# The gated stage's first product in 2x2 blocks: seven block products instead of eight

## The chip, the cores and the metric

The kernel runs on one NeuronCore of a Trainium2 chip. The metric is the device time of one execution in microseconds (us). The engines are TensorE (PE in the rows, with its weight loads as PEld), VectorE (DVE), ScalarE (ACT), GpSimd (POOL) and SyncE (SP), which here only issues transfers. Each engine takes its instructions in the order in which the program lists them.

## What is computed

Three layers follow one another on 8 sequences of 576 tokens with 512 features: an attention by landmarks, a mixing layer (Fourier transform, normalization, two products with 2048 hidden features), and the gated layer that the change touches. Of the reference, cut to that layer:

```python
B, S, D = x.shape                       # 8, 576, 512;  d_ff = 1024
x_prev = np.concatenate([np.zeros((B, 1, D)), x[:, :-1, :]], axis=1)
xk = mu_k * x + (1.0 - mu_k) * x_prev
xr = mu_r * x + (1.0 - mu_r) * x_prev
k = np.maximum(xk @ w_k, 0.0)           # first product
v = k * k @ w_v                         # second product
r = 1.0 / (1.0 + np.exp(-(xr @ w_r)))   # gate
return r * v
```

## The kernel before

The 4608 tokens are worked in 9 blocks of 512. Two stages follow one another. In the first, the attention of the 8 sequences (`batch`) is laid between the products of the mixing layer (`block_a`, 9 blocks). In the second, the gated stage, a class `Gated` holds one block's work.

Every number that goes into a product is held as two fp16 halves, high and low, and each product is made of three matmuls (`PARTS`: high by high, high by low, low by high). The first product of a block is `first(f)` for f = 0 to 7: 128 of the 1024 hidden features, 4 chunks of the 512 input features, 3 parts, so 12 matmuls of 128x512 into one PSUM bank (`ph`, two banks in turn). ScalarE evacuates the bank with a Relu (`rk`), VectorE squares, ScalarE and VectorE split the square into halves (`k2`). `second(f)` takes them up two steps later with 12 matmuls into the four `acc` banks, and `gate(j)` is 12 more, four times a block, into a bank of the pool `gp`. At the end of a block VectorE multiplies each `acc` by the gate (`o`), and it is stored. `prep(i)` makes the operands `xk` and `xr` of a block: it loads `yb`, squares (`sq`), sums over features through four transposes, gets a power of two as scale, spreads it by four more transposes (`rs`), mixes each token with the one before it (`xt`), and splits the result into halves.

The weights come as 64 bit floats. In the first stage `Weights.run` takes apart a piece of 128x512 of them at a time (tile `wst`; three ScalarE and two VectorE instructions), and keeps `w_k`, `w_v` and `w_r` as fp16 halves in HBM; the gated stage loads them back.

The order on each engine is not the order of the code. A class `Plan` records all instructions, and `issue()` lists them by a planner with costs of its own (`Engine.cost`): at each point an engine takes the instruction that the planner holds ready and that has the longest way to the end (`key`, to which `iss.lead` adds: `NOW` for the stage's products, `SOON` for `prep`, 0 for the far weights). The block matmuls alone keep the order of the code (`chain=True`). The lines 333 (matmul), 349 (transpose), 317 (DMA) and 188 (the other engines) in the rows are those of helpers, so instructions are told apart by their tiles.

Of the kernel before, what the change touches and what calls it, by code (L numbers as in the profile page):

```python
# [11 lines left out]
F32 = mybir.dt.float32  # L12
# [11 lines left out]
DM = H * D  # L24
# [500 lines left out]
class Weights:  # L525
# [11 lines left out]
    def clear(self, x):  # L537
        self.iss.g.memset(x, 0)
        return x

    def run(self, src, hi, lo, room=None):

# [502 lines left out]
def build(nc, tc, a):  # L1045
# [5 lines left out]
    with stack, tc.manual_schedule():  # L1051
# [67 lines left out]
            w12_items += [piece("w_ch2", f, 0, w2, f) for f in range(4 * g, 4 * g + 4)]  # L1119


        shapes = {"w_k": [128, 2, 4, FF2], "w_v": [128, 2, 8, DM], "w_r": [128, 2, 4, DM]}
        kept = {
            n: iss.dram(tc.dram_tile(x, F16, name="d" + n), x, F16, "d" + n)
            for n, x in shapes.items()
# [6 lines left out]
                kept[name][:, :, rows, c:c + WCH],  # L1132
            )

        far_items = [far("w_k", c, g) for g in range(2) for c in range(4)]
        far_items += [far("w_v", f, 0) for f in range(8)] + [far("w_r", c, 0) for c in range(4)]

        def tmp(name="tmp"):
            return iss.tile(com, [128, 512], F32, name, "tmp", 3)
# [146 lines left out]
        for n, x in enumerate(w12_items):  # L1286
            weights.run(*x, room=rooms[n % 3] if n < 24 else None)
        iss.lead = 0.0
        for x in far_items:
            weights.run(*x)  # L1290
        iss.slack = 0.0
# [14 lines left out]
        wk, wv, wr = ([ws[n][:, x] for x in range(2)] for n in ("w_k", "w_v", "w_r"))  # L1306
        mus = iss.tile(pb, [128, 4, 4], F32, "mus")
        iss.load(mus[:, 0], a["mu_k"])
        iss.load(mus[:, 1], a["mu_r"])
# [2 lines left out]

        def prep(i):
            iss.lead = SOON
            pool, nb, nx = (pb2, 2, 8) if i else (pb, 1, 4)
            y = iss.tile(pool, [128, 4, BLK + 1], F32, "yb", bufs=nb)
            if i == 0:
                g_.memset(y[:, :, 0:1], 0.0)
                iss.load(y[:, :, 1:], ys[:, :, 0:BLK])
            else:  # L1320
                iss.load(y, ys[:, :, BLK * i - 1:BLK * i + BLK])
            q = None
            for c in range(0, 4, 2):
                pair = []
                for d in (c, c + 1):
                    pair.append(iss.tile(pool, [128, BLK + 1], F32, "sq", bufs=3))
# [30 lines left out]
            xk = [iss.tile(pool, [128, 4, BLK], F16, "xk", f"xk{x}", nb) for x in "hl"]  # L1357
            xr = [iss.tile(pool, [128, 4, BLK], F16, "xr", f"xr{x}", nb) for x in "hl"]
            for c in range(4):
                for n, x in enumerate((xk, xr)):  # L1360
                    t = iss.tile(pool, [128, 512], F32, "xt", bufs=nx)
                    s_.activation(t, y[:, c, 0:BLK], AF.Copy, scale=mus[:, 2 + n, c:c + 1])
                    if i < B:
                        g_.memset(t[:, o:o + 1], 0.0)
                    v_.scalar_tensor_tensor(
                        t, y[:, c, 1:], mus[:, n, c:c + 1], t, op0=ALU.mult, op1=ALU.add
                    )
                    v_.tensor_tensor(t, t, rs, op=ALU.mult)
                    s_.activation(x[0][:, c], t, AF.Copy)
                    g_.tensor_tensor(x[1][:, c], t, x[0][:, c], op=ALU.subtract)  # L1370
            return xk, xr, nz, qi

        class Gated:


            def __init__(self, i):
                self.i = i
# [14 lines left out]
                s_.activation(e, ps, AF.Sigmoid, scale=self.nz[:, j:j + 1])  # L1392
                self.sg.append(e)

            def first(self, f):
                iss.lead = NOW
                ps = ph()
                sl = slice(128 * f, 128 * f + 128)
                for c in range(4):
                    for n, (x, y) in enumerate(PARTS):  # L1400
                        mm(
                            ps, wk[x][:, c, sl], self.xk[y][:, c],
                            c == 0 and n == 0, c == 3 and n == 2, chain=True,
                        )
                rk = iss.tile(pb2, [128, 512], F32, "rk", bufs=3)
                s_.activation(rk, ps, AF.Relu, scale=1.0 / (4 * WS))
                k2 = iss.tile(pb2, [128, 2, 512], F16, "k2", bufs=4)
                v_.tensor_tensor(rk, rk, rk, op=ALU.mult)
                s_.activation(k2[:, 0], rk, AF.Copy)
                v_.tensor_tensor(k2[:, 1], rk, k2[:, 0], op=ALU.subtract)  # L1410
                self.ks[f] = k2

            def second(self, f):
                iss.lead = NOW
                if f == 0:
                    self.acc = acc_banks()
                k2 = self.ks.pop(f)
                for j in range(4):
                    sl = slice(128 * j, 128 * j + 128)
                    for n, (x, y) in enumerate(PARTS):  # L1420
                        mm(
                            self.acc[j], k2[:, x, sl], wv[y][:, f],
                            f == 0 and n == 0, f == 7 and n == 2, chain=True,
                        )
                if f < 7:
                    return
                for j in range(4):
                    o = iss.tile(pb2, [128, 512], F32, "o", bufs=3)
# [5 lines left out]
                    iss.load(a["out"][r0:r0 + 128, :], o)  # L1434


        blocks = {}
        for n in range(8 * NB + 2):
            i, f = divmod(n, 8)
            if i < NB:  # L1440
                if f == 0:
                    blocks[i] = Gated(i)
                blocks[i].first(f)
            if n >= 2:
                blocks[(n - 2) // 8].second((n - 2) % 8)
            if i < NB and 1 <= f < 5:
                blocks[i].gate(f - 1)
        iss.issue()


# [87 lines left out]
```

## Time and profile before

| | |
|---|---|
| median of three runs | 1510.58 us (1510.31 to 1510.58) |
| span of the profiled execution | 1508.6 us |
| instructions on the engines | 21555 |
| busy PE / PEld / DVE / ACT / POOL | 1495.0 / 734.4 / 822.5 / 601.2 / 291.2 us |
| the gated stage, first to last matmul | 1028.9 to 1503.9 us |

The span is from the first to the last instruction in the trace; no device time of its own is listed for the profiled execution, and the median lies 2.0 us above its span. Matmuls are pipelined, and a row's duration of one matmul overlaps the next one's, so their pace is read from the starts of two runs of matmuls in a timeline and not from the mean duration.

### The profile page before, as it was taken

The page shows a single profiled execution, that of the slowest core. Times are in us where ns is not written, and L with a number is a line of the kernel's source. Part 1 is how long each engine was busy: PE and PEld are TensorE (multiplying, and loading weights), DVE is VectorE, ACT ScalarE, POOL GpSimd, SP SyncE. Part 2 cuts the span into 40 slices and gives each one's busy share as a digit, 9 for nine tenths or more (in the row PEclk, how much of TensorE's full clock was granted, in tenths as well). Part 3 has the DMA queues.
Part 4 walks back from the last instruction along what each step waited for, and adds up shares of the span by engine and source line. Part 5 has one row for each costly group of instructions (what it writes and reads, how often), then busy time and mean ns, then how long its engine had stood idle before and what let it go on. Part 6 is the DMA issues. An engine that isn't in the chain of part 4 may idle for free.

```text
span 1508.6 us, 21555 instructions
## 1 busy us (share of the span) xinstructions
PE 1495.0 (99%) x8541; PEld 734.4 (49%) x8541; DVE 822.5 (55%) x1732; ACT 601.2 (40%) x1257; POOL 291.2 (19%) x355
## 2 busy tenths in 40 slices
PE   9999999999999999999999999999999999999998
PEld 5554455554545545545544444444444444444443
DVE  7877685766756446545343352214777765662222
ACT  4666545445343322323322231115555554343221
POOL 3012121121201201201202130002544442131000
PEclk9999999999999999999999999999999999999999
DMA  8353242433231101000004000002101101000000
GB/s 292 111 174 127 83 151 84 147 102 116 85 105 64 33 28 64 32 29 1 1 28 168 28 1 1 28 1 84 57 29 56 57 29 57 28 22 8 28 28 28
DMA packets 43731, 97.89 MB, mean 65 GB/s; under 512 B 4208, under 2 KB 9584, under 8 KB 43120
## 3 DMA queue, kind: packets, MB, share of 16 engines
q1 hardware_dynamic: 43632, 96.53, 18.5%
q8 instruction: 67, 1.10, 0.3%
q14 instruction: 32, 0.26, 0.1%
HBM read 72.40 MB, written 24.12 MB: 64 GB/s over the span
## 4 chain that ended last, share of the span: by engine, by line
PE 96%; DVE 2%; ACT 1%; issue 0%; POOL 0%; DMA 0%; DVEq 0%; POOLq 0%
PE acc L333 37%; PE ph L333 37%; PE gp L333 18%; PE gp L349 3%; PE spare L1097 1%; DVE small L188 1%; PE acc L1097 0%; ACT Y L188 0%; DVE bdY L188 0%; DVE uc L188 0%; DMA out<-o 0%; DVE un L188 0%; DVE w1l L188 0%; DVE tmp L188 0%; DVE bdR L188 0%
## 5 line engine op out<-in xcount | busy, mean ns | idle before, releaser
L333 PE MATMUL ph<-un,w1h 128*128 128x512 f16 x1152 | 350.6, 379 | 0.1
L333 PE MATMUL acc<-h,w2h 128*128 128x512 f16 x1152 | 349.6, 379 | 0.4 <-ACT w2h L188 0.4
L188 DVE SCALAR_TENSOR_TENSOR h<-ph,h 128x512 f16<-128x512 f32 x144 | 99.0, 688 | 234.9 <-ACT h L188 234.4
L333 PE MATMUL ph<-un,w1l 128*128 128x512 f16 x576 | 218.5, 379 | 0.8 <-DVE w1l L188 0.8
L333 PE MATMUL acc<-h,w2l 128*128 128x512 f16 x576 | 218.6, 379 | 0.3 <-DVE w2l L188 0.3
L188 ACT ACTIVATE h<-ph 128x512 f16<-128x512 f32 x144 | 85.9, 596 | 298.6 <-PE ph L333 298.0
L333 PE MATMUL ph<-xk,w_k 128*128 128x512 f16 x864 | 199.6, 379 | 0.0
L333 PE MATMUL acc<-w_v,k 128*128 128x512 f16 x864 | 198.9, 379 | 0.0
L333 PEld LDWEIGHTS <-w2h 128*128 128x128 f16 x1152 | 113.0, 99 | 127.7 <-issue 7.4
L333 PEld LDWEIGHTS <-w1h 128*128 128x128 f16 x1152 | 112.2, 99 | 127.6 <-issue 11.9
L188 DVE TENSOR_TENSOR rk<-rk 128x512 f32<-128x512 f32 x72 | 55.4, 770 | 146.3 <-ACT rk L188 146.0
L333 PEld LDWEIGHTS <-k 128*128 128x128 f16 x864 | 84.5, 98 | 100.6
L333 PEld LDWEIGHTS <-w_k 128*128 128x128 f16 x864 | 84.5, 98 | 99.7
L333 PE MATMUL gp<-w_r,xr 128*128 128x512 f16 x432 | 99.3, 379 | 0.7 <-ACT rs L188 0.7
L188 ACT ACTIVATE rk<-ph 128x512 f32<-128x512 f32 x72 | 42.9, 596 | 129.3 <-PE ph L333 121.5
L333 PEld LDWEIGHTS <-w1l 128*128 128x128 f16 x576 | 57.0, 99 | 67.2 <-issue 7.5
L333 PEld LDWEIGHTS <-w2l 128*128 128x128 f16 x576 | 57.0, 99 | 66.6 <-issue 7.4
L188 DVE TENSOR_TENSOR k<-rk,k 128x512 f16<-128x512 f32 x72 | 59.3, 823 | 29.2 <-ACT k L188 29.0
L188 POOL TENSOR_TENSOR sq<-sq 128x513 f32<-128x513 f32 x27 | 36.8, 1362 | 198.9 <-ACT sq L188 198.3
L188 POOL TENSOR_TENSOR xr<-xt,xr 128x512 f16<-128x512 f32 x36 | 48.6, 1372 | 112.1 <-ACT xr L188 112.1
L333 PEld LDWEIGHTS <-xr 128*128 128x128 f16 x432 | 42.3, 98 | 51.4 <-issue 0.9
L188 DVE TENSOR_TENSOR xt<-xt,rs 128x512 f32<-128x512 f32 x72 | 60.4, 868 | 2.9 <-ACT rs L188 2.8
(171 smaller groups left out, 1869.6 us busy)
## 6 DMA issues: line engine op xcount, KB each, us to landing
wst<-in_w_ch SPq DMA_DIRECT2D x24, 512.0 KB, 3.8
q<-in_q SPq DMA_DIRECT2D x16, 578.0 KB, 4.8
k<-in_k SPq DMA_DIRECT2D x16, 576.0 KB, 4.8
ys<-ub SPq DMA_DIRECT2D x36, 256.0 KB, 2.1
out<-o SPq DMA_DIRECT2D x36, 256.0 KB, 2.0
yb<-ys SPq DMA_DIRECT2D x8, 1026.0 KB, 5.1
v<-in_v SPq DMA_DIRECT2D x8, 1024.0 KB, 6.4
more<-in_w_ch SPq DMA_DIRECT2D x8, 512.0 KB, 4.3
```

The costliest lines, as they stand in the source:

```text
L188: f(real(out), *map(real, args), **{k: real(x) for k, x in kw.items()})
L333: self.nc.tensor.matmul(out.real(), lhsT=lhsT.real(), rhs=rhs.real(), start=start, stop=stop, **kw)
L349: self.nc.tensor.transpose(out.real(), in_.real(), ident.real())
L1097: nc.tensor.matmul(into.real() if into else spare[0], lhsT=z.to_broadcast([128, 128]), rhs=z.to_broadcast([128, 512]), start=not into, sto ...
```

## The change

The first product of a block becomes a product of 2x2 blocks. The weight is cut into halves of the input features (256) and, inside each group `g` of 512 hidden features, into halves of 256; the tokens of a block are cut into two halves of 256. Seven block products of sums and differences then give the four output blocks, where eight would be needed without sums. Each block product is 2 feature tiles by 2 chunks by 3 parts, 12 matmuls of 128x256, and there are 7 of them for each of two groups of a block.

Three things go with it. `Weights.pair` makes the four sums of the weight's blocks on GpSimd when the weights are taken apart, and `w_k` is kept as 7 blocks. `prep` makes four differences of the tokens' blocks on VectorE and splits 7 blocks into halves instead of 4 chunks; `yb` has one buffer in place of two. And the group's seven products use banks that stay open: product after product is added into the same bank (`px`, then `py`), and ScalarE or VectorE reads the partial sum between two of them. A generator yields where such a read is due, and a `second` or a `gate` is put there (`fillers`); the first group of the first block has only two gates to put there. Squares and halves are now made from the sums (`out`).

```diff
+    def pair(self, srcs, dram):
...
+        (a, e0), (b, e1) = [self.single(x, self.tops[0]) for x in srcs]
...
+        g_.tensor_tensor(s1, a[:, w], b[:, w], op=ALU.add)
+        g_.tensor_tensor(s2, s1, a[:, u], op=ALU.subtract)
+        g_.tensor_tensor(s3, a[:, u], a[:, w], op=ALU.subtract)
+        g_.tensor_tensor(s4, b[:, u], s2, op=ALU.subtract)
+        for x, at in ((a[:, u], 0), (b, 1), (e0, 3), (e1, 5)):
+            n = wide(x) // h
+            both = iss.tile(self.pool, [128, 2, n, h], F16, "wboth", "wtop1")
+            xs = x.rearrange("p (n f) -> p n f", n=n)
+            s_.activation(both[:, 0], xs, AF.Copy, scale=WS)
+            v_.scalar_tensor_tensor(
+                both[:, 1], xs, WS, both[:, 0], op0=ALU.mult, op1=ALU.subtract
+            )
+            iss.load(dram[:, :, at:at + n], both)
...
-        shapes = {"w_k": [128, 2, 4, FF2], "w_v": [128, 2, 8, DM], "w_r": [128, 2, 4, DM]}
+        shapes = {"w_k": [128, 2, 7, 2, FF2 // 2], "w_v": [128, 2, 8, DM], "w_r": [128, 2, 4, DM]}
...
-            pool, nb, nx = (pb2, 2, 8) if i else (pb, 1, 4)
-            y = iss.tile(pool, [128, 4, BLK + 1], F32, "yb", bufs=nb)
+            pool, nb = (pb2, 2) if i else (pb, 1)
+            y = iss.tile(pool, [128, 4, BLK + 1], F32, "yb", bufs=1)
...
+            (b11, b12), (b21, b22) = ts
+            split(0, b11)
+            split(1, b21)
+            v_.tensor_tensor(b11, b12, b11, op=ALU.subtract)
+            split(2, b22)
+            v_.tensor_tensor(b12, b22, b12, op=ALU.subtract)
+            v_.tensor_tensor(b22, b22, b11, op=ALU.subtract)
+            split(5, b22)
+            split(4, b11)
+            v_.tensor_tensor(b21, b21, b22, op=ALU.subtract)
+            split(6, b12)
+            split(3, b21)
...
-            def first(self, f):
+            def first(self, g):
...
+                def product(ps, w, b, opens):
+                    for f in range(2):
+                        o = 256 * g + 128 * f
+                        for c in range(2):
+                            for n, (x, y) in enumerate(PARTS):
+                                mm(
+                                    ps[:, HB * f:HB * f + HB], wk[x][:, w, c, o:o + 128],
+                                    xk[y][:, b, c], opens and f == 0 and c == 0 and n == 0,
+                                    c == 1 and n == 2, chain=True, skip_group_check=True,
+                                )
...
+                def out(t, a, z):
+
+                    v_.scalar_tensor_tensor(t, t, 0.0, t, op0=ALU.max, op1=ALU.mult)
+                    t = t.rearrange("p (f n) -> p f n", f=2)
+                    hi, lo = [k2[:, x, 2 * a:2 * a + 2, HB * z:HB * z + HB] for x in range(2)]
+                    scale = (1.0 / (4 * WS)) ** 2
+                    s_.activation(hi, t, AF.Copy, scale=scale)
+                    v_.scalar_tensor_tensor(lo, t, scale, hi, op0=ALU.mult, op1=ALU.subtract)
+
+                px, py = ph(), ph()
+                product(px, 0, 0, True)
+                product(py, 3, 4, True)
+                t1 = copy(px)
+                yield
+                product(px, 4, 5, False)
+                t2 = copy(px)
+                yield
+                product(px, 5, 6, False)
+                t3 = copy(px)
+                v_.tensor_tensor(t3, py, t3, op=ALU.add)
+                yield
+                product(px, 2, 3, False)
+                t4 = copy(px, AF.Relu)
+                out(t3, 1, 1)
+                out(t4, 1, 0)
+                product(py, 6, 2, False)
+                v_.tensor_tensor(t2, py, t2, op=ALU.add)
+                yield
+                pz = ph()
+                assert pz.tile.bank == px.tile.bank
+                product(pz, 1, 1, True)
+                v_.tensor_tensor(t1, pz, t1, op=ALU.add)
+                out(t1, 0, 0)
+                out(t2, 0, 1)
+                yield
+                yield
...
+        def fillers(n):
+
+            i, g = divmod(n, 2)
+            late = []
+            if n:
+                u, p = divmod(n - 1, 2)
+                late = [partial(blocks[u].second, f) for f in Gated.order[4 * p:4 * p + 4]]
+            if i == NB:
+                return late
+            gates = [partial(blocks[i].gate, 2 * g + j) for j in range(2)]
+            return gates if not late else late[0:2] + gates[0:1] + late[2:4] + gates[1:2]
```

What this makes of the order is seen at two places. The first is TensorE in the first group of the first block, from its fourth block product (into `px`, behind the second gate) to the first one of the second group. Of the change, the rows that wait (a block product is 12 pairs of load and matmul; the first row of each block product is among those shown):

```order
L333 MATMUL ph<-xk,w_k 128x256 [waits Activation_49]
L333 LDWEIGHTS w_k
L333 MATMUL ph<-xk,w_k 128x256 [waits Pool_49]
...
L333 MATMUL ph<-xk,w_k 128x256 [waits Activation_49]
...
L333 MATMUL ph<-xk,w_k 128x256 [waits DVE_49]
...
L333 MATMUL ph<-xk,w_k 128x256 [waits Activation_49]
...
L333 MATMUL ph<-xk,w_k 128x256 [waits DVE_49]
```

And of before, the same stretch, from the third product of the first block on into the first `second`:

```order
L333 MATMUL gp<-w_r,xr 128x512
L333 LDWEIGHTS w_k
L333 MATMUL ph<-xk,w_k 128x512 [waits Activation_49]
L333 LDWEIGHTS w_k
L333 MATMUL ph<-xk,w_k 128x512
...
L333 MATMUL acc<-w_v,k_9522 128x512
L333 LDWEIGHTS k_9522 [waits DVE_49]
```

Before, a product waits once, for the evacuation of a bank that was filled two products earlier; now a product that is added to an open bank waits for the read of what the product before it left there, and at this place the two stand directly behind one another.

The second place is VectorE in the second group of the second block (`xt_10087` and `xt_10100` are the chunk pairs of `xk` of the third block; `rk<-ph,rk` is a sum read from a bank). With the change:

```order
L188 TENSOR_SCALAR small<-small 128x4 x3
L188 SCALAR_TENSOR_TENSOR xt_10100<-yb,mus,xt_10100 128x512 x2
L188 SCALAR_TENSOR_TENSOR xt<-yb,mus,xt 128x512
L188 TENSOR_TENSOR xt_10087<-xt_10087,rs 128x512 x2
L188 TENSOR_TENSOR xt_10100<-xt_10100,rs 128x512 x2
L188 TENSOR_TENSOR xt<-xt,rs 128x512
L188 TENSOR_TENSOR xt_10087<-xt_10087 128x2x256
L188 TENSOR_TENSOR xt_10087<-xt_10100,xt_10087 128x2x256
L188 TENSOR_TENSOR rk<-ph,rk 128x512
L188 SCALAR_TENSOR_TENSOR rk<-rk 128x512
```

And a stretch of before in which `prep` is likewise mixed in:

```order
L188 TENSOR_TENSOR k_10075<-rk,k_10075 128x512
L188 SCALAR_TENSOR_TENSOR xt<-yb,mus,xt 128x512
L188 TENSOR_TENSOR xt<-xt,rs 128x512 x2
L188 SCALAR_TENSOR_TENSOR xt<-yb,mus,xt 128x512 x2
L188 TENSOR_TENSOR rk<-rk 128x512
L188 SCALAR_TENSOR_TENSOR xt<-yb,mus,xt 128x512 x2
L188 TENSOR_TENSOR k_10160<-rk,k_10160 128x512
```

Before, VectorE's work on `rk` came after ScalarE had emptied the bank. Now one of these instructions, the sum `rk<-ph,rk`, itself reads the bank, and a row of mixing instructions stands ahead of it in the queue.

## Rows read from the trace of the kernel before

**Rows 1.** The page: busy time by engine; granted TensorE clock in 40 slices.

```profile
PE 1495.0 (99%) x8541; PEld 734.4 (49%) x8541; DVE 822.5 (55%) x1732; ACT 601.2 (40%) x1257; POOL 291.2 (19%) x355
PEclk9999999999999999999999999999999999999999
```

**Rows 2.** Busy time in one window, the gated stage (columns PE, PEld, DVE, ACT, POOL, clock, DMA).

```profile
1028.90:1503.90 475.00, 473.72 (x2225) 218.70 (x2223) 259.12 (x373) 206.50 (x349) 135.85 (x159) 1.00 0.11 38
```

**Rows 3.** Timeline near the stage's end: start, duration, engine, work, count, [idle before].

```profile
1487.97 2.47 PEld L333 LDWEIGHTS <-w_k 128*128 128x128 f16 x12
1488.18 2.75 PE L333 MATMUL ph<-xk,w_k 128*128 128x512 f16 x12
...
1490.77 2.75 PE L333 MATMUL acc<-w_v,k 128*128 128x512 f16 x12
1491.03 0.60 ACT L188 ACTIVATE rk<-ph 128x512 f32<-128x512 f32 x1 [3.20 <-PE ph L333]
```

**Rows 4.** Timelines of shorter matmuls and their weight loads, in both stages.

```profile
735.03 2.40 PE L333 MATMUL gp<-c_cosT,Ae 96*128 96x289 f16 x18
...
737.92 2.30 PEld L333 LDWEIGHTS <-Ao 96*128 96x128 f16 x18
...
1049.00 0.57 PEld L349 LDWEIGHTS gp<-ident,s 128*128 128x128 f32 x4
...
1049.22 0.60 PE L349 MATMUL gp<-ident,s 128*128 128x128 f32 x4
```

**Rows 5.** Groups of instructions in the gated stage: busy us, mean ns, idle before.

```profile
L333 PE MATMUL ph<-xk,w_k 128*128 128x512 f16 x864 | 199.6, 379 | 0.0
...
L188 DVE TENSOR_TENSOR k<-rk,k 128x512 f16<-128x512 f32 x72 | 59.3, 823 | 29.2 <-ACT k L188 29.0
L188 DVE TENSOR_TENSOR rk<-rk 128x512 f32<-128x512 f32 x72 | 55.4, 770 | 146.3 <-ACT rk L188 146.0
L188 DVE TENSOR_TENSOR xt<-xt,rs 128x512 f32<-128x512 f32 x64 | 54.4, 876 | 1.5 <-ACT rs L188 1.4
L188 DVE SCALAR_TENSOR_TENSOR xt<-yb,mus,xt 128x512 f32<-128x512 f32 x64 | 52.0, 836 | 1.4 <-POOL xt L188 1.1 <-ACT xt L188 0.3
...
L188 POOL TENSOR_TENSOR xk<-xt,xk 128x512 f16<-128x512 f32 x32 | 44.1, 1396 | 40.6 <-ACT xk L188 40.4
...
L188 DVE SCALAR_TENSOR_TENSOR o<-acc,qi,sg 128x512 f32<-128x512 f32 x35 | 24.8, 745 | 21.8 <-PE acc L333 21.8
...
L188 ACT ACTIVATE rs<-gp 128x512 f32<-128x512 f32 x8 | 4.8, 597 | 7.3 <-PE gp L349 7.3
```

**Rows 6.** TensorE's waits in the whole span: us in total, times, longest.

```profile
PE gp L349 <- DVE small L188: 1.8, 3, 0.8
...
PE gp L333 <- ACT rs L188: 0.7, 1, 0.7
```

**Rows 7.** Timeline at the stage's start.

```profile
1028.93 5.34 PE L333 MATMUL ph<-xk,w_k 128*128 128x512 f16 x24
1032.29 0.60 ACT L188 ACTIVATE rk<-ph 128x512 f32<-128x512 f32 x1 [7.74 <-DMA ys<-ub]
...
1047.40 0.18 POOL L188 COPY s<-sq 128x1 f32<-128x1 f32 x1
```

**Rows 8.** Taking weights apart: its instructions, their window, and a GpSimd row of that window.

```profile
L188 ACT ACTIVATE wboth<-wst x20: 640/662/677, 229.5 to 447.4; 128x512 f16<-128x512 f32 x20
L188 DVE SCALAR_TENSOR_TENSOR wboth<-wst,wboth x20: 675/682/1037, 230.2 to 449.5; 128x512 f16<-128x512 f32 x20
...
190.00:300.00 110.00, 109.35 (x810) 58.45 (x809) 76.25 (x205) 54.74 (x134) 17.47 (x21) 1.00 0.41 126
...
L188 POOL TENSOR_TENSOR Ae<-d,Ae 97x256 f16<-97x256 f32 x3 | 2.0, 668 | 3.7 <-ACT Ae L188 3.7
```

**Rows 9.** Transfers: issues, KB, us to landing; and the one load of `w_k`.

```profile
L317 SPq DMA_DIRECT2D w_k<-dw_k x1: 430/430/430, 793.5 to 793.5; - x1
...
w_k<-dw_k SPq DMA_DIRECT2D x1, 2048.0 KB, 9.7
...
yb<-ys SPq DMA_DIRECT2D x8, 1026.0 KB, 5.1
```

More of the change, by code (lines that the diff above doesn't have):

```diff
@@ L1133, in far, with far_pair @@
             )
-        far_items = [far("w_k", c, g) for g in range(2) for c in range(4)]
-        far_items += [far("w_v", f, 0) for f in range(8)] + [far("w_r", c, 0) for c in range(4)]
+        def far_pair(name, c, g):
+            col = 2 * WCH * g
+            h = WCH // 2
+            return (
+                [a[name][128 * r:128 * r + 128, col:col + 2 * WCH] for r in (c, c + 2)],
+                kept[name][:, :, :, c, h * g:h * g + h],
+            )
+        far_pairs = [far_pair("w_k", c, g) for g in range(2) for c in range(2)]
+        far_items = [far("w_v", f, 0) for f in range(8)] + [far("w_r", c, 0) for c in range(4)]
         def tmp(name="tmp"):
@@ L1288, in build @@
         iss.lead = 0.0
+        for x in far_pairs:
+            weights.pair(*x)
         for x in far_items:
@@ L1356, in prep, with mixed @@
             s_.activation(rs, rb, AF.Copy)
-            xk = [iss.tile(pool, [128, 4, BLK], F16, "xk", f"xk{x}", nb) for x in "hl"]
+            xk = [iss.tile(pool, [128, 7, 2, HB], F16, "xk", f"xk{x}", nb) for x in "hl"]
             xr = [iss.tile(pool, [128, 4, BLK], F16, "xr", f"xr{x}", nb) for x in "hl"]
-            for c in range(4):
[L1360 to L1370, printed above, removed]
+            def mixed(t, n, c):
+                s_.activation(t, y[:, c, 0:BLK], AF.Copy, scale=mus[:, 2 + n, c:c + 1])
+                if i < B:
+                    g_.memset(t[:, o:o + 1], 0.0)
+                v_.scalar_tensor_tensor(
+                    t, y[:, c, 1:], mus[:, n, c:c + 1], t, op0=ALU.mult, op1=ALU.add
+                )
+                v_.tensor_tensor(t, t, rs, op=ALU.mult)
@@ new lines, in split @@
+            def split(at, t):
+                s_.activation(xk[0][:, at], t, AF.Copy)
+                g_.tensor_tensor(xk[1][:, at], t, xk[0][:, at], op=ALU.subtract)
+            ts = []
+            for c in (0, 2):
+                t = iss.tile(com, [128, 2, BLK], F32, "xt2", "wst", 2)
+                for d in range(2):
+                    mixed(t[:, d], 0, c + d)
+                ts.append([t[:, :, 0:HB], t[:, :, HB:]])
+            (b11, b12), (b21, b22) = ts
+            split(0, b11)
@@ L1371, in prep @@
             return xk, xr, nz, qi
         class Gated:
+            order = [2, 3, 0, 1, 6, 7, 4, 5]
             def __init__(self, i):
@@ L1393, in gate, with room, copy @@
                 self.sg.append(e)
-            def first(self, f):
+            def first(self, g):
                 iss.lead = NOW
[L1397 to L1411, printed above, removed]
+                xk = self.xk
+                k2 = iss.tile(pb2, [128, 2, 4, BLK], F16, "k2", bufs=2)
+                self.ks[g] = k2
+                def product(ps, w, b, opens):
[7 more added lines that the diff above has]
+                                    c == 1 and n == 2, chain=True, skip_group_check=True,
+                                )
+                def room():
+                    return iss.tile(pb2, [128, 512], F32, "rk", bufs=6)
+                def copy(ps, func=AF.Copy):
+                    t = room()
+                    s_.activation(t, ps, func)
+                    return t
+                def out(t, a, z):
[32 more added lines that the diff above has]
+                yield
@@ L1421, in second @@
                         mm(
-                            self.acc[j], k2[:, x, sl], wv[y][:, f],
-                            f == 0 and n == 0, f == 7 and n == 2, chain=True,
+                            self.acc[j], k2[:, x, f % 4, sl], wv[y][:, f],
+                            opens and n == 0, closes and n == 2, chain=True,
                         )
-                if f < 7:
+                if not closes:
                     return
@@ L1434, in second @@
                     iss.load(a["out"][r0:r0 + 128, :], o)
+        def fillers(n):
[8 more added lines that the diff above has]
+            return gates if not late else late[0:2] + gates[0:1] + late[2:4] + gates[1:2]
         blocks = {}
-        for n in range(8 * NB + 2):
-            i, f = divmod(n, 8)
+        for n in range(2 * NB + 1):
+            i, g = divmod(n, 2)
+            steps = iter(())
             if i < NB:
-                if f == 0:
+                if g == 0:
                     blocks[i] = Gated(i)
[L1443 to L1447, printed above, removed]
+                steps = blocks[i].first(g)
+            todo = fillers(n)
+            for _ in steps:
+                if todo:
+                    todo.pop(0)()
+            for x in todo:
+                x()
         iss.issue()
```

42 lines of the change are left out of this document (38 added, 4 removed).

## Prediction

> **What bounds the kernel now.** I read the page's busy times first: TensorE is busy 99% of the span, no other engine over 55%, and the granted clock is in the top tenth in all 40 slices [rows 1]; in the stage it is 1.00 of 2.4 GHz [rows 2]. Then the window of the gated stage, 475.0 us with TensorE busy 473.7 of them, VectorE 259, ScalarE 207, GpSimd 136 [rows 2]. TensorE's own waits are a few tenths of a us here and there [rows 6]. So the kernel ends when TensorE has gone through its list, and each us of matmuls taken out is a us won, as long as nothing new makes TensorE wait.
>
> The mean of 379 ns of a matmul is not its pace. In the timeline twelve matmuls of the first product start at 1488.18 and the next twelve at 1490.77: 2.59 us, so 215.8 ns each [rows 3]. That is 512 columns at 2.4 GHz (213.3 ns) and 2.5 ns. The twelve weight loads in front of them begin 0.21 us ahead, take about 98 ns each and spread over the same 2.5 us: they lie under the matmuls before them [rows 3].
>
> **What the change removes.** 864 matmuls of 512 columns in the first product [rows 5], 864 x 0.2158 = 186.4 us.
>
> **What it adds on TensorE.** 9 blocks x 2 groups x 7 products x 12 = 1512 matmuls of 256 columns. The trace has no fp16 matmul of that length. Two neighbours bound it. Eighteen matmuls of 289 columns take 2.40 us, the last one's 287 ns included, so (2.40 - 0.29)/17 = 124.3 ns each [rows 4]; less 33 columns at 2.4 GHz that is 110.5. Four fp32 transposes of 128 columns take 0.60 us, (0.60 - 0.273)/3 = 109 ns each, with weight loads of over 100 ns under them [rows 4]; twice 128 columns at 2.4 GHz are 106.7, so they seem to be streamed twice. The load, 98 ns, is shorter than either. I take 110: 166.3 us added (164.8 to 167.1), so TensorE's list is shorter by 20.1 us (19.3 to 21.6).
>
> The Trainium skill speaks against this sum in "TensorE: Matmul & The Clock Gate", Part 3, The mechanism: a weight load overlaps a matmul in flight only when the two use different row groups. Here all use all rows, and the trace disagrees: 98 ns of load plus 213 of streaming would be 311 ns each, and 215.8 is measured [rows 3]. By the page the change would be a loss; by the rows a gain of 20.
>
> **Waits for open banks.** Four times in a group a product has to wait for ScalarE's copy of what the last one left in the bank. From the rows: ScalarE starts the copy 0.26 us after TensorE has moved on (1491.03 against 1490.77), and takes 0.60 [rows 3]; with some 0.1 for the way back TensorE can go on after 0.95. A filler of 12 matmuls is 2.59 us, so 1.6 us are left over. VectorE's sum `py + t3` needs 0.75 more (the nearest rows are 745 and 770 ns [rows 5]), but a filler and a product of 1.32 us lie over it.
>
> In the first group of the first block there are only two fillers. There product 2 follows product 5 directly and waits 0.95; the next three waits have a product of 1.32 us over them, and only the last, behind two VectorE sums and a square, comes out some 0.2 late. I take 1.2 us. The first copy there waits for the last store of the first stage, as it does now (1032.29, 3.4 us after the stage's start [rows 7]); product 4 comes 5.2 us after the start, so this stays hidden.
>
> **VectorE in the other groups.** Per block the five large kinds cost 8 x (0.823 + 0.770 + 0.876 + 0.836) + 4 x 0.745 = 29.4 us now [rows 5]. With the change: 6 sums (0.75), 8 squares (0.77), 8 low halves (0.823), 4 differences (0.876), the 16 mixing instructions and 4 `o` as they are: 4.5 + 6.2 + 6.6 + 3.5 + 13.7 + 3.0 = 37.5, of a block of 50 us. Not the bound on average, but in the second group of a block the mixing stands ahead of the sum that TensorE waits for. That walk, from the group's start: the scale's transposes are done at 3.1, `rs` (0.597 [rows 5]) at 3.9; five multiplications and two differences take 7 x 0.876 = 6.1, to 10.0; product 5 ends at 10.9, its copy at 11.9 with the way, the sum at 12.7; the product that needs it is due at 14.8. So 2 us are spare: VectorE's eight instructions in that walk may each be 0.25 us longer, for GpSimd's sake or another, before TensorE waits. The other sums have 4 us and more. Bounds: nothing, and one uncovered evacuation in each of 17 groups, 16 us. I take 2.0 in all, near the lower end, because the walk leaves slack and the present stage has waits of 0.8 us at most [rows 6].
>
> **`prep` with one `yb`.** The next load can begin only when the last mixing instruction has read `yb`; it lands 5.1 us later [rows 9]. GpSimd gets three more splits a block at 1.4 us [rows 5], so 136/8 + 4.2 = 21 us of 50. For the second block, `prep` starts with the stage, and in the trace its sums leave GpSimd 18.7 us after the stage's start [rows 7]; with the change TensorE reaches the transposes that need them after nine products, two gates and ten matmuls, 19.2 us plus the waits above. Tight, but even: part of the 2.0.
>
> **The first stage.** `w_k` now costs 16 instructions of 256 columns on GpSimd (nearest row 668 ns, so 11 us), and on ScalarE and VectorE 16 instructions each for 8, of which 12 are as long as before: some 4 us each (660 and 680 ns a piece [rows 8]). In the 110 us where this falls VectorE is busy 76, ScalarE 55, GpSimd 17 [rows 8]: there is room for it. SP issues 16 stores for 8, with the loads of later sequences among them as before. What stands behind all these is the attention of later sequences, whose matmuls TensorE takes in a fixed order. Lower bound 0, upper bound two or three waits of 0.8 us [rows 6]; I take 0.5. `w_k` comes back as 3.5 MB instead of 2, some 17 us for 10, but at 793 us, 235 us before its use [rows 9]: nothing.
>
> **Sum.** -20.1 + 1.2 + 2.0 + 0.5 = -16.4 us. The profiled span is 1508.6 and becomes 1492.2; the runs' median lies 2.0 above the span, so **1494.2 us**. A difference of 0.2% (3 us) is about what a measurement of this kernel can tell from no change.
>
> **Rivals.**
> - *Evacuation late in many groups.* For it: VectorE at 75% of a block with its large instructions alone, and only 1.6 and 2 us of slack behind queues that neither engine can reorder. Against it: the walk. At 0.6 us in each of 17 groups it costs 10 us in place of 2: 1502.
> - *`prep` becomes the bound (slower).* With one `yb`, load, squares, sums, transposes, mixing, differences and splits of a block follow one another, and the next block's first product waits for them. It decides from 2.0 us late per block on (16.4 over 8 blocks). For it: the mixing fills most of VectorE's second half of a block. Against it: ScalarE, VectorE and GpSimd have some 25, 12 and 28 of 50 us free, and the differences needed last are used 10 us into the next block. At 4 us late per block: 1494 + 32 = 1526.
> - *Loads no longer hidden (slower).* From 186.4/1512 = 123.3 ns per matmul on, TensorE gains nothing. If load and matmul of 256 columns follow one another (98 + 107 = 205 ns), 1512 x 0.205 = 310: 1494 + 144 = 1638. Against it: both neighbours in rows 4. This is the page's rule above.
> - *A shorter matmul that does not shrink by half.* If its pace is 118 ns for another reason (the 289 columns have 3.9 ns above their streaming, the 512 have 2.5), 178.4 us are added: 1506, and half the work of the change is lost.
>
> **Chances.** Forecast (1490 to 1499) 0.64; late evacuation (1499 to 1507) 0.19; pace of 118 0.04; `prep` 0.10; loads 0.03. Below 1489.0, the list shorter by 21.6 us and no wait at all, I see no mechanism. The range 1489 to 1506 leaves out the two slower cases and the end of the late ones. Faster by over 0.2%: 0.64 + 0.17 + 0.02 = 0.83; within it 0.04; slower 0.13.
>
> **What would show it.** In the changed profile: 1512 matmuls of 256 columns, twelve of them in 1.31 to 1.33 us from start to start; the stage's window at 455 to 460 us; one gap of about 1 us some 11 us into it, ended by ScalarE's `rk`; waits of `ph` for `rk` of ScalarE and VectorE of less than 2 us elsewhere. The rival on evacuation would show as many waits of `ph` for `rk`, the one on `prep` as waits for `xk` at a block's first products or for `small` and `s` at the transposes, the ones on the pace as starts 118 ns or more apart with no idle time. I am wrong if TensorE's waits in the stage add up to more than 8 us, or if the first stage ends more than 3 us later than 1028.9.

## The result and the profile after

The changed kernel takes 1493.78 us (median of four runs, 1491.53 to 1494.1) against 1510.58: a ratio of 0.9886, 95% interval 0.9872 to 0.9900. The forecast was 1494.2. The run of 1491.53 us had a mean granted clock of 0.998, the other three (1493.57 to 1494.1 us) one of 0.995 to 0.997.

The page of the changed kernel, with its busy times and the granted clock (before: [rows 1]):

```profile
span 1492.3 us, 23013 instructions
PE 1476.0 (99%) x9189; PEld 798.9 (54%) x9189; DVE 906.2 (61%) x1830; ACT 619.1 (41%) x1292; POOL 341.6 (23%) x398
PEclk9999999999999999999999999999999999999999
```

Windows of the changed kernel: the stage, 286 us of it without the start, and four stretches in its second block (columns as in [rows 2]).

```profile
1028.20:1487.60 459.40, 455.19 (x2874) 282.93 (x2871) 329.87 (x459) 218.44 (x373) 170.23 (x183) 0.99 0.11 40
...
1200.00:1486.00 286.00, 286.00 (x1801) 176.60 (x1800) 199.15 (x284) 128.64 (x221) 99.77 (x99) 1.00 0.10 36
...
1084.00:1088.00 4.00, 2.00 (x9) 1.24 (x9) 0.41 (x2) 3.97 (x7) 2.45 (x4) 0.55 0.01 2
1088.00:1092.00 4.00, 4.00 (x21) 2.60 (x19) 1.59 (x3) 3.08 (x6) 1.91 (x3) 0.60 0.00 0
...
1084.00:1084.50 0.50, 0.00 (x0) 0.00 (x0) 0.03 (x1) 0.50 (x2) 0.00 (x0) 0.91 0.00 0
...
1084.50:1091.00 6.50, 5.00 (x23) 3.30 (x23) 1.41 (x2) 5.55 (x11) 3.44 (x6) 0.50 0.00 1
```

The stage lasts 459.4 us for 475.0 [rows 2]. VectorE has 330 us of work in it for 259, ScalarE and GpSimd have more too, and yet from 1200 us on TensorE is busy without a gap. The time that it does wait lies in two places near the stage's start. At the second one the granted clock falls to half while TensorE still stands (0.91 in the half us from 1084.0 on, then 0.50) and stays there until 1091. In the page's 40 slices that is not to be seen: the tenths still read 9.

TensorE's timeline at both places (columns as in [rows 3]):

```profile
1028.26 2.78 PE L333 MATMUL ph<-xk,w_k 128*128 128x256 f16 x24
1030.88 2.75 PE L333 MATMUL gp<-w_r,xr 128*128 128x512 f16 x12
1033.47 1.47 PE L333 MATMUL ph<-xk,w_k 128*128 128x256 f16 x12
1034.78 2.75 PE L333 MATMUL gp<-w_r,xr 128*128 128x512 f16 x12
1037.37 1.47 PE L333 MATMUL ph<-xk,w_k 128*128 128x256 f16 x12
1039.53 2.67 PE L333 MATMUL ph<-xk,w_k 128*128 128x256 f16 x23 [0.69 <-ACT rk L188]
...
1079.55 2.32 PE L333 MATMUL gp<-w_r,xr 128*128 128x512 f16 x10
1082.15 0.61 PE L333 MATMUL gp<-w_r,xr 128*128 128x512 f16 x2 [0.28 <-POOL xr L188]
1085.14 0.37 PE L333 MATMUL ph<-xk,w_k 128*128 128x256 f16 x1 [2.38 <-ACT xk L188]
1086.38 5.03 PE L333 MATMUL ph<-xk,w_k 128*128 128x256 f16 x23 [0.86 <-POOL xk L188]
1091.23 2.76 PE L333 MATMUL acc<-w_v,k 128*128 128x512 f16 x12
```

Twenty-four matmuls of 256 columns take 2.62 us from start to start (1028.26 to 1030.88), 109.2 ns each; twelve take 1.31 (1033.47 to 1034.78). The wait for an open bank is the gap ahead of 1039.53: the product before began at 1037.37 and had its pace until 1038.68, so 0.85 us are lost. At 1086.38 twenty-three matmuls take 4.85 us and not 23 x 0.1092 = 2.51: that is the halved clock, 2.3 us. The waits of this place, with the one inside the gate before it, are 0.44 us (ahead of 1082.15), 2.55 and 1.12, together 4.1 from start to start.

What the 2.38 us at 1085.14 waited for, in the timeline of all engines of the changed kernel:

```profile
1081.23 1.41 DVE L188 SCALAR_TENSOR_TENSOR rk<-rk 128x512 f32<-128x512 f32 x1
1082.57 0.68 DVE L188 TENSOR_TENSOR xt<-xt 128x512 f32<-128x512 f32 x1
1082.68 0.63 ACT L188 ACTIVATE k<-rk 128x512 f16<-128x512 f32 x1 [1.81 <-DVE rk L188]
1083.37 0.63 ACT L188 ACTIVATE sq<-yb 128x513 f32<-128x513 f32 x1
1083.90 0.67 ACT L188 ACTIVATE sg<-gp,nz 128x512 f32<-128x512 f32 x1
1084.47 0.62 ACT L188 ACTIVATE xk<-xt 128x512 f16<-128x512 f32 x1
1085.17 1.15 POOL L188 TENSOR_TENSOR xk<-xt,xk 128x512 f16<-128x512 f32 x1 [3.07 <-ACT xk L188]
```

This is the last of the second block's differences, the operand of the fifth of its group's seven block products, `product(px, 2, 3)`. VectorE makes it at 1082.57 behind a square; ScalarE could make its high half from 1083.25 on, but has a square of the third block's `prep` and a sigmoid ahead of it in its queue, and comes to it at 1084.47; GpSimd's low half follows at 1085.17. TensorE had nothing else to do from 1082.58 on, so the difference was late before ScalarE's queue made it later.

### The profile page after: what moved, and what is told of

Its sections match the earlier page's. It is cut to its first block, busy times and chain, and to the rows that moved or that the text cites. A ratio compares the mean times of both kernels' runs of the same rounds, so it can differ in the third digit from the quotient of the medians.

```text
span 1492.3 us, 23013 instructions
## 1 busy us (share of the span) xinstructions
PE 1476.0 (99%) x9189; PEld 798.9 (54%) x9189; DVE 906.2 (61%) x1830; ACT 619.1 (41%) x1292; POOL 341.6 (23%) x398
## 4 chain that ended last, share of the span: by engine, by line
PE 95%; DVE 2%; ACT 1%; DMA 1%; issue 0%; POOL 0%; DVEq 0%; ACTq 0%; POOLq 0%
PE acc L333 37%; PE ph L333 36%; PE gp L333 18%; PE gp L349 3%; PE spare L1142 1%; DMA dw_k<-wboth 0%; DVE small L188 0%; DMA yb<-ys 0%; PE acc L1142 0%; ACT Y L188 0%; DVE uc L188 0%; DVE bdY L188 0%; DVE bdR L188 0%; DMA out<-o 0%; DVE un L188 0%
## 5 line engine op out<-in xcount | busy, mean ns | idle before, releaser
L333 PE MATMUL ph<-xk,w_k 128*128 128x256 f16 x1512 | 183.7, 275 | 3.9 <-ACT xk L188 2.4
L333 PEld LDWEIGHTS <-w_k 128*128 128x128 f16 x1512 | 149.0, 99 | 40.9 <-issue 4.7
L188 POOL TENSOR_TENSOR xk<-xt,xk 128x512 f16<-128x512 f32 x63 | 86.6, 1386 | 130.0 <-ACT xk L188 129.2
L188 DVE TENSOR_TENSOR rk<-ph,rk 128x512 f32<-128x512 f32 x54 | 37.2, 689 | 88.9 <-ACT rk L188 62.0
L188 ACT ACTIVATE k<-rk 128x512 f16<-128x512 f32 x72 | 44.8, 627 | 83.4 <-DVE rk L188 83.4
L188 DVE SCALAR_TENSOR_TENSOR rk<-rk 128x512 f32<-128x512 f32 x72 | 71.3, 1004 | 3.2 <-ACT rk L188 2.2
L188 DVE SCALAR_TENSOR_TENSOR xt<-yb,mus,xt 128x512 f32<-128x512 f32 x72 | 60.2, 870 | 13.0 <-POOL xt L188 7.4
```

Source lines behind the costliest of these rows:

```text
L188: f(real(out), *map(real, args), **{k: real(x) for k, x in kw.items()})
L333: self.nc.tensor.matmul(out.real(), lhsT=lhsT.real(), rhs=rhs.real(), start=start, stop=stop, **kw)
```

## The experiments

All ratios are to the kernel before, with 95% intervals. Where an edit stands on the changed kernel, its time to compare with is 1493.8 us.

**The pace alone (e3_before_256).** The kernel before, with each matmul of the first product split in two of 256 columns:

```diff
-                for c in range(4):
-                    for n, (x, y) in enumerate(PARTS):
-                        mm(
-                            ps, wk[x][:, c, sl], self.xk[y][:, c],
+                for z in range(2):
+                    h = slice(256 * z, 256 * z + 256)
+                    for c in range(4):
+                        for n, (x, y) in enumerate(PARTS):
+                            mm(
+                                ps[:, h], wk[x][:, c, sl], self.xk[y][:, c, h],
...
```

> The kernel before, each matmul of 512 columns in the first product as two of 256, eight products' worth of columns, nothing else. Theory (256 columns take 109.2 ns, that is streaming and 2.5 ns, the weight load hidden): 1728 x 109.2 - 864 x 215.8 = 2.3 us more than before, 1512 to 1513.5 us. Rival (short matmuls pay for their loads, and the seven products save more than their share): 1515 us or more.

Measured: 1512.7 us, ratio 1.0013 (1.0004 to 1.0022). Its group of the first product, and its timeline:

```profile
L333 PE MATMUL ph<-xk,w_k 128*128 128x256 f16 x1728 | 201.8, 273 | 0.0
```

```profile
1036.33 2.78 PE L333 MATMUL ph<-xk,w_k 128*128 128x256 f16 x24
1038.95 2.75 PE L333 MATMUL acc<-w_v,k 128*128 128x512 f16 x12
1041.54 2.75 PE L333 MATMUL gp<-w_r,xr 128*128 128x512 f16 x12
```

24 in 2.62 us again, 109.2 ns for 215.8/2 = 107.9 (12 in 2.59). Twice as many instructions and loads cost 1728 x 1.3 ns = 2.2 us, and 2.1 are measured. A matmul of half the length costs half but for 1.3 ns, and its load (98 ns) stays hidden.

**The reads of open banks (e4_no_fillers).** No `second` and no `gate` is put where a generator yields; they follow the group:

```diff
-                if todo:
-                    todo.pop(0)()
+                pass
```

> The changed kernel with the seven block products of a group directly behind one another, and the second products and gates after them. Theory (a read of an open bank costs TensorE 0.85 to 0.95 us where no other work lies over it): two such reads in each group, 1.7 to 1.9 us in 17 groups and one more in the first, 1523 to 1530 us, slower than before. Rival (reads of the open bank cost nothing, the other engines' queues are what counts): 1490 to 1497 us.

Measured: 1520.5 us, ratio 1.0068 (1.0055 to 1.0082): 26.7 us above the changed kernel, and slower than before. Its waits of TensorE (columns as in [rows 6]):

```profile
PE ph L333 <- ACT rk L188: 25.2, 36, 1.2
```

Thirty-six waits over 18 groups, mostly two in each: 0.7 us each in this view, 0.85 from start to start. The change pays only because other matmuls lie over these reads. The time is below the expected 1523 to 1530 us although the two bare reads in a group came as expected: the expectation kept the late place of the second block, and here only 1.4 us of waiting are left of its 4.1, with the clock at 1.00.

**The weights' sums (e6_no_sums).** The four sums on GpSimd left out:

```diff
-        g_.tensor_tensor(s1, a[:, w], b[:, w], op=ALU.add)
-        g_.tensor_tensor(s2, s1, a[:, u], op=ALU.subtract)
-        g_.tensor_tensor(s3, a[:, u], a[:, w], op=ALU.subtract)
-        g_.tensor_tensor(s4, b[:, u], s2, op=ALU.subtract)
-        for x, at in ((a[:, u], 0), (b, 1), (e0, 3), (e1, 5)):
+        for x, at in ((a[:, u], 0), (b, 1), (a, 3), (b, 5)):
```

> The changed kernel without the sixteen GpSimd sums of the weights' blocks: four of the seven blocks of w_k are then plain pieces, so this part of the computation is left out and its time alone is read. Theory (the first stage has room for them, as the stage's start shows): within 1 us of the changed kernel, 1492.5 to 1494.5 us, the stage starting at 1028 to 1029 us. Rival (they hold up the attention that stands behind them on GpSimd): 1 us or more faster, the stage starting earlier.

Measured: 1493.1 us (1492.4 to 1493.5), ratio 0.9886 (0.9869 to 0.9902); the changed kernel's own runs spread over 2.6 us, so this is no difference that can be told. The gated stage starts at 1027.60 us here and at 1028.26 in the changed kernel, but in the other kernels that have the sums it starts anywhere from 1027.44 to 1028.70. So the first stage hides the sums, as far as this can be read.

**The halved clock (e5_zeros_in_gap).** Twelve matmuls of zeros, added to a bank of `acc`, are put into the late place, ahead of the late product; they change no value:

```diff
+                if g == 0 and self.i == 1:
+                    for _ in range(12):
+                        mm(
+                            blocks[0].acc[0], zero[:, 0:1].to_broadcast([128, 128]),
+                            zero[:, 0:1].to_broadcast([128, 512]), False, False,
...
                 product(px, 2, 3, False)
```

> The changed kernel with twelve matmuls of zeros, added into an open accumulation bank, ahead of the block product of the second block that is late; they change no value. They take 2.6 us of the 3.7 us that TensorE idles there. Theory (the place costs 4 us of waiting and a further 2.4 us of halved clock after it): the waiting ends when it did, but the clock stays at 2.4 GHz, 1490.8 to 1492 us, and the runs lie closer together than the 2.6 us of the changed kernel. Rival (the fall of the clock has nothing to do with the idle time, or costs nothing): 1493.5 to 1496 us.

Measured: 1491.2 us (1490.2 to 1491.5), ratio 0.9872 (0.9858 to 0.9887), 2.6 under the changed kernel. Its timeline of TensorE, and the two instructions that split the late operand:

```profile
1082.84 2.78 PE L333 MATMUL acc<-zero 128*128 128x512 f16 x12
1085.46 0.27 PE L333 MATMUL ph<-xk,w_k 128*128 128x256 f16 x1
1085.93 2.67 PE L333 MATMUL ph<-xk,w_k 128*128 128x256 f16 x23 [0.20 <-POOL xk L188]
1088.44 2.75 PE L333 MATMUL acc<-w_v,k 128*128 128x512 f16 x12
```

```profile
1084.03 0.62 ACT L188 ACTIVATE xk<-xt 128x512 f16<-128x512 f32 x1
...
1084.72 1.16 POOL L188 TENSOR_TENSOR xk<-xt,xk 128x512 f16<-128x512 f32 x1 [2.38 <-ACT xk L188]
```

The same 23 matmuls now take 2.51 us for 4.85, which is 2.3 us of clock. The rest is not the clock: with the zeros in it the planner's list has ScalarE's square behind the split, and counted from the stage's start (1028.49 us here, 1028.26 there) GpSimd's half begins 0.7 us earlier. So the edit changes a second thing, and the matmuls are what shows the price of the clock: the place is 4.1 us of waiting with some 2.4 of clock on top.

**What makes the place late (e1_gates_last, e2_xk_first, e9_second_block_ahead).** Three ways to give the operand more time. e1 puts the gates of a block's first group behind all four `second` of it:

```diff
-            return gates if not late else late[0:2] + gates[0:1] + late[2:4] + gates[1:2]
+            return late + gates if not g else late[0:2] + gates[0:1] + late[2:4] + gates[1:2]
```

> Theory: in the changed kernel TensorE loses some 4 us at one place, the second block's product with the block of tokens that prep makes last, and 2.4 us more because its clock falls there. Here the two gates of a block's first group come after all four second products, so the mixing for xr is needed later and VectorE's list makes the last difference of xk ahead of it: the place loses under 1 us, the clock stays at 2.4 GHz, 1487 to 1489 us. Rival (VectorE as a whole is too slow for prep in the first block): the wait only moves to the gate or to another product, 1492 to 1495 us.

Measured: 1491.3 us (1491.2 to 1491.6), ratio 0.9873 (0.9858 to 0.9888). Its waits show that the late place is gone, and what came for it:

```profile
PE gp L333 <- ACT sg L188: 2.3, 3, 0.8
```

Two gates now stand side by side in every block, and in three of them the second waits for the sigmoid that empties its bank. That I had not expected; it takes back 2.8 us, start to start, and the time lies above the 1487 to 1489 us of the theory.

e2 leaves TensorE's order alone and lets the planner list the differences and splits of `xk` earlier, in all blocks:

```diff
+            iss.lead = NOW
             split(0, b11)
...
             split(3, b21)
+            iss.lead = SOON
```

> Only the other half: the differences and halves of xk get the priority of the products, the gates stay where they are. Theory (order of VectorE's list at this place): the block of xk is in time, but the first gate needs all four chunks of xr, which now come later, so a wait of 2 to 4 us stands at the gate; 1490 to 1494 us. Rival (the last difference alone is what is late, nothing else near it is tight): 1487 to 1489 us.

Measured: 1489.3 us (1488.8 to 1489.9), ratio 0.9859 (0.9846 to 0.9873). Its waits, and its window at the place:

```profile
PE gp L333 <- POOL xr L188: 1.6, 2, 0.8
```

```profile
1084.00:1088.00 4.00, 4.00 (x30) 2.74 (x28) 2.40 (x3) 4.00 (x8) 2.12 (x3) 1.00 0.01 2
```

The wait has moved to the gates' operands ahead of it and is half as long, 1.9 us start to start; the clock stays at 1.00. That is 2.2 + 2.4 = 4.6 us, and 4.4 are measured. The wait that the theory named did come, a little smaller than it said, and the time falls just below its range.

e9 lists the whole preparation of the second block earlier, and of no other:

```diff
-            iss.lead = SOON
+            iss.lead = NOW if i == 1 else SOON
```

> All of the second block's preparation is listed at the place where it is asked for and not a little later; all else as in the changed kernel. Theory that the late place in the second block (4.1 us, and 2.4 us of halved clock behind it) comes of where the list puts that preparation: it shrinks to 2 us or less, the granted clock stays up, 1488.5 to 1490.5 us, as e2. Rival: VectorE has no time left in the first block, so that what is listed earlier only pushes the reads of the first block's sums back: waits of 2 us or more for rk or acc in the first block, 1491.5 to 1495.

Measured: 1489.1 us (1488.7 to 1489.4), ratio 0.9859 (0.9842 to 0.9875). One wait of 1.4 us, start to start, is left there:

```profile
PE ph L333 <- ACT rk L188: 1.9, 2, 1.3
```

So the second block's preparation was late by its place in the queues. The rival, that VectorE has no time for it, falls: the same VectorE work is done, in another order, and TensorE gets its operands.

**The first group's 0.85 us (e7_gates_spread, e8_first_gates, e10_fourth_tile, e11_ahead_and_first_gates).** All four give the first block's four gates to its first group, so that each read has matmuls over it. e7 and e8 stand on e2; e7 also moves gates of the later blocks' first groups back by a `second`. e8's edit:

```diff
-            gates = [partial(blocks[i].gate, 2 * g + j) for j in range(2)]
-            return gates if not late else late[0:2] + gates[0:1] + late[2:4] + gates[1:2]
+            mine = range(2 * g, 2 * g + 2) if i else range(4 - 4 * g)
+            gates = [partial(blocks[i].gate, j) for j in mine]
+            return late[0:2] + gates[0:1] + late[2:4] + gates[1:2] if late else gates
```

> The priority of e2 for xk, all four gates of the first block between the products of its first group, and in every other first group the gates after the third and the fourth second product, with other work between them. Theory: the 0.85 us at the first block's third product, the 1.9 us at the gate of e2 and the 0.94 us between the adjacent gates of e1 all go, 1486 to 1488 us, the stage with less than 1 us of idle time. Rival (VectorE cannot make xk and xr of the second block in time whatever the order): 1489 us or more.

> Keeps e2's order in the preparation and moves one more thing: the first block has its four gates in its first group, between the first products and their sums; every other block's gates stay where e2 has them. Theory that the 0.85 us wait of the stage's first group is only for want of other matmuls between the products and the block product that overwrites a read bank: it goes and nothing else moves, e2's 1489.3 less 0.85, 1488.0 to 1488.9 us. Rival, as in e7: the gates taken out of the first block's second group leave that place bare, and a wait of the same size or more comes there or in the second block: 1489.5 to 1493.

Measured: e7 1492.8 us, ratio 0.9883 (0.9869 to 0.9898); e8 1493.8, 0.9890 (0.9875 to 0.9904). In both the first group's wait is gone and a longer one came, at a gate of the second block: 4.1 us in two waits in e7 and 5.0 in e8, start to start. In both the granted clock fell there too (e8: 0.76 from 1081.4 to 1088 us). For e8 this is the place that its rival named, with a time above the rival's range. e7's rival said that VectorE cannot be in time whatever the order, and e9 shows that it can. Of e8, the waits, and ScalarE's timeline ahead of them:

```profile
PE gp L333 <- ACT xr L188: 3.5, 1, 3.5
...
PE gp L333 <- POOL xr L188: 1.2, 1, 1.2
```

```profile
1079.31 0.60 ACT L188 ACTIVATE rk<-ph 128x512 f32<-128x512 f32 x1 [2.84 <-PE ph L333]
1079.80 0.71 ACT L188 ACTIVATE xt<-yb,mus 128x512 f32<-128x512 f32 x1
...
1082.65 0.63 ACT L188 ACTIVATE xr<-xt 128x512 f16<-128x512 f32 x1 [0.63 <-DVE xt L188]
```

ScalarE stood idle for 2.84 us because the head of its queue was a read of a bank not yet filled. Whether the step of `prep` behind it could have gone at once, this does not show. To see whether a buffer holds that step, e10 takes e8 with four `xt` for three and five `rk` for six:

```diff
-                t = iss.tile(pool, [128, 512], F32, "xt", bufs=3 if i else 2)
+                t = iss.tile(pool, [128, 512], F32, "xt", bufs=4 if i else 2)
...
-                    return iss.tile(pb2, [128, 512], F32, "rk", bufs=6)
+                    return iss.tile(pb2, [128, 512], F32, "rk", bufs=5)
```

> As e8, with four buffers in place of three for the normalised chunk xt, and five in place of six for the sums rk. Theory that what is left of the second block's lateness (gaps of 1.0 and 0.9 us at the gates in e2) is the wait of the fourth chunk for a buffer of the first: these gaps shrink under 0.5 us in all and the time is 1 to 1.5 us under e8's. Rival: the chunk's chain through ScalarE and GpSimd is the limit and not the buffer: within 0.5 us of e8's. Third: five rk buffers are too few, TensorE waits for rk in groups of two or more later blocks, and the time is over e8's.

Measured: 1495.6 us, ratio 0.9901 (0.9886 to 0.9916). It is worse, at the same gates (waits for `xr` of 2.5 us of GpSimd and 1.9 of ScalarE), not at `rk` of later blocks, so neither the first nor the third theory came. But the edit changes two counts of buffers at once and the clock falls for longer than in e8 (0.70 from 1081.4 to 1088 us, 0.64 in the next 4 us, for 0.76 and 0.97), so what the fourth buffer alone is worth stays open. The last one joins e8's gates to e9's earlier preparation (both edits as above):

> e9's edit (the whole preparation of the second block listed earlier) and e8's (the first block's four gates in its first group) together. In e8 the second block's third chunk was normalised by ScalarE only at 1079.8 us, behind a read of sums that waits for its product; e9 has the same step at 1070.8. Theory that the list's place of that step was e8's cause and nothing about the gates: here the first group's wait of 0.85 us goes without another coming, e9's 1489.1 less 0.85, 1487.7 to 1488.7 us. Rival: the first block's second group without gates stays bare whatever the preparation does, and 2 us or more are waited at its end or in the second block: 1489.5 to 1493.

Measured: 1491.1 us (1490.4 to 1491.9), ratio 0.9873 (0.9856 to 0.9889). The gates have their operands now, but one wait of 3.9 us came at the second block's open bank (and one of 0.7 us for `xk`, 300 us later), so the rival's range holds:

```profile
PE ph L333 <- ACT rk L188: 3.9, 1, 3.9
```

ScalarE's queue is at fault again, the other way round: the read of the bank, at 1084.39, stands behind four squares, a split, a sigmoid and three mixing steps, and the first of these squares waited 1.4 us for its load. The clock stayed up all the same. An order that spares both waits was not found; the best kernels stay e2 and e9, within 0.3 us of each other.

## Why the prediction was right

- **What bounds the kernel.** Right: TensorE is busy 99% after as before, and 15.6 of the 16.3 us came off the stage (459.35 us for 474.96, first start to last end).
- **The list, -20.1.** 110 ns a matmul was 0.8 too dear; at 109.2 the 1512 cost 165.1 us and the list is 21.3 shorter. The nearer neighbour of [rows 4] was the fp32 one at 109. By the Trainium skill, "TensorE: Matmul & The Clock Gate", Part 3, The mechanism, a load overlaps a matmul in flight only when the row groups differ, so it would not overlap here; the trace of e3 disagrees as the one of before did: 98 ns of load under matmuls of 109.2. The same section also lets a load into the background weight buffer go ahead, which the prediction did not say; no run here shows where a load goes.
- **First group, +1.2.** Measured 0.85, at the place and by the engine named. Only the first wait came; the last one, put at 0.2, stayed covered.
- **The other groups, +2.0.** The size is wrong by a factor of three, and so is the picture. Seventeen groups have no wait at all for a read; ScalarE and VectorE come in time. Instead one place in the second block, whose `prep` the text called tight, costs 4.1 us, and the halved clock 2.4. The walk through VectorE's queue was made for the reads, and the second block's operands were followed only as far as their sums; the last difference was not followed through VectorE's queue, where it was made only when TensorE was already free for it, nor its split through ScalarE's, where it lost another 1.2 us. A fall of the clock had no term at all. The squares, priced at 770 ns, took 1004 on average, and the one ahead of the late difference took 1410.
- **The first stage, +0.5.** It ends 0.7 us earlier (1028.26 against 1028.93 [rows 7]), which is within what this start moves from kernel to kernel, and e6 shows that the sums cost nothing that can be told.
- **The sum.** -21.3 + 0.85 + 4.1 + 2.4 - 0.7 = -14.6 us. The two waits that TensorE had in the stage of before are gone, 0.74 and 0.85 us from start to start, and the prediction had no term for that; in the timeline of before:

```profile
1050.73 1.46 PE L333 MATMUL gp<-w_r,xr 128*128 128x512 f16 x6
1052.77 0.62 PE L349 MATMUL gp<-ident,small 128*128 128x128 f32 x4 [0.58 <-DVE small L188]
...
1202.41 0.60 PE L349 MATMUL gp<-ident,small 128*128 128x128 f32 x4
1203.69 0.59 PE L333 MATMUL gp<-w_r,xr 128*128 128x512 f16 x2 [0.68 <-ACT rs L188]
```

  That makes -16.2, for -16.3 between the spans. So the total is close by luck, by errors that cancel: a list 1.2 us shorter, a first group 0.35 and a first stage 1.2 better and 1.6 of old waits gone, against 4.5 more at the second block. Of my bounds for being wrong, 8 us of waits in the stage, 5.0 were reached.
- **The rivals.** Late evacuation in many groups did not come; e4 shows what it would have cost, 27 us more than the change with two bare reads in each group. `prep` is not the bound: it was late in one block only, and from 1200 us on TensorE has no gap. The loads are hidden and the pace is no 118 (e3).

## What to carry to other kernels

Where a product can be cut to fewer matmuls of half the length, measure the pace of the short ones first: one kernel that only splits the old ones (e3) decides most of it. Here a partial sum could be read from an open bank at no cost where a product of something else lay over the read; each bare read cost 0.85 us. Then follow every operand of the first blocks through all queues that it passes, since the loss here was one late place, with the clock's price on top, and moving it in the list (e2, e9) was worth 4.4 to 4.7 us more. Giving the first group more cover as well (e7, e8, e11) lost more at the next place than it won.

## What the hardware showed that I had not expected

- **The clock.** In the changed kernel TensorE had waited 0.44 us, done two matmuls and then stood still from 1082.58 us on when the granted clock fell from 1.00 to 0.50, at about 1084.4; it rose again at about 1091.2. Matmuls that take 109.2 ns at the upper level (2.4 GHz) took 213 at the lower one (1.2 GHz; eighteen in 3.84 us from 1086.75 on). It fell in e6, e7, e8 and e10 as well, all of which have two or more waits close together in the second block. In e8 it was still at 1.00 through 3.6 us without work, and fell only at the end of a second wait, of 1.3 us. In e9, after a gap of 1.4 us, and in e2, after 1.0 and 0.9, it stayed at 1.00; and so it did in e11, though TensorE stood still for 4.0 us from start to start. The window of e11 that holds that gap:

```profile
1081.40:1088.00 6.60, 2.97 (x26) 2.53 (x26) 2.96 (x4) 6.10 (x12) 6.38 (x11) 1.00 0.00 1
```

  So the length of a gap alone does not say when the clock falls: it fell 1.9 us into one and not in one of 4.0. What else decides stays open.
- **VectorE's operands.** Durations of two kinds of its instructions in the stage of the changed kernel, least/median/most in ns:

```profile
L188 DVE SCALAR_TENSOR_TENSOR rk<-rk x72: 673/692/1761, 1040.2 to 1472.8; 128x512 f32<-128x512 f32 x72
...
L188 DVE TENSOR_TENSOR rk<-ph,rk x54: 673/691/693, 1039.5 to 1472.1; 128x512 f32<-128x512 f32 x54
```

The squares, which read SBUF twice, average 1004 ns where I had priced 770; thirty of the 72 take over 800, and each of these lies beside a GpSimd instruction on two tensors (five more lie beside one and take 707 at most). The sums that read one operand from a PSUM bank never take over 693 ns, though 32 of the 54 lie beside such a GpSimd instruction. The Trainium skill, "SBUF — State Buffer", section Who interferes with whom, says that a VectorE instruction with two SBUF inputs contends with a GpSimd one that reads SBUF, and one with a single SBUF input, outside VectorE's two-port modes, does not; the trace agrees. So the sum that TensorE waits for, read from the open bank, was of the kind that GpSimd did not slow here.
